# Queries of eight attention units loaded in 128-byte runs and turned by VectorE in SBUF instead of by TensorE

## The chip, the cores and the metric

The kernel runs on one core of a Trainium2 chip. The metric is device time in microseconds (us) of one execution. All engines of the core take part: TensorE (matmuls and, by a matmul with the identity, transposes), VectorE and ScalarE (elementwise work and the way out of PSUM), GpSimd and SyncE (which issue transfers to the 16 DMA engines).

## What is computed

Three stages follow one another: packed attention, a gated mixer, and a channel mixer. Cut to what matters:

```python
# attention, for each of 8 batches and 8 heads: q, k, v are [576, 64], p is [32, 64]
p_packed = sm_attn(p, k, v)                 # 32 packed rows look at all keys
out = sm_attn(q, p_packed, p_packed)        # every query looks at the 32 packed rows
# sm_attn(q, k, v): softmax(q k^T / sqrt(64)) v

# mixer on x = [8, 576, 512], x_prev = x moved down by one row
xk = mu_k * x + (1 - mu_k) * x_prev
xr = mu_r * x + (1 - mu_r) * x_prev
k = relu(xk @ w_k); v = (k * k) @ w_v; r = sigmoid(xr @ w_r); x = r * v

# channel mixer
u = x + (x^T @ U @ V)^T
out = u + relu(u @ w_ch1) @ w_ch2
```

## The kernel before

The kernel is written as a list of operations that a planner (`Plan`) puts in order. Each operation names its engine or engines, what it reads and writes, and a class. `emit` then runs through the list with a cost for each operation and hands every engine, whenever it is free, the ready operation of the lowest class; TensorE and SyncE take the oldest of a class, the others the one that was ready first. `copy` may go to ScalarE or to VectorE, whichever comes free for it first. The order that results is fixed in the program, and each engine runs its own list strictly in order. So a change of one step moves others around it. SyncE's list holds nearly all transfers; a transfer that waits for its data holds those behind it.

The attention is cut into 16 units. Unit u takes two heads (j = u % 4) of two batches (pair bp = u // 4). Units 0 to 7 (`NPLAIN = 8`, called plain) run at the start of the program, on four sets of buffers. Units 8 to 15 run on one set, one after another, beside the chunks of the mixer: the loop over chunks (n = 2 to 11; 384 columns each, three for each pair of batches) puts the units of pair 2 ahead of chunk 2 and those of pair 3 ahead of chunk 5. The pair's mixer chunks come only later, so the units are side work; the chunks' matmuls (`psr`, `psk`, `psv` for the products with w_r, w_k and w_v, `psu` for U) fill TensorE between their steps. Weights of the last stage are also loaded and prepared in the background there (`st`, `w_d`, class 3). From about 703 us on the last stage runs (`psc`, `psh`, `pst`).

A unit (`attention_steps`, L648) goes through these steps:

- k is turned by TensorE (`kin` to `kh`), scores of the packed rows are made (`sps`), and VectorE takes their maxima into `st` with two reductions; ScalarE takes exponentials into `a1`.
- q is turned. `load_q` (L621) brings q of both batches into `qin`, 128 partitions of 1152 values: partition 2p + b2 holds nine rows of both heads of batch b2. Two transfers of 288 KB do that, in runs of one row of a head, 64 values or 256 bytes. Then in three steps three blocks of 128x128 each are turned by TensorE into PSUM (bank `psat`), and a copy on ScalarE or VectorE brings each bank into `qt`, where a partition is a value of a head and the columns are the queries.
- the packed values (`pp`, `ppt`) are made from `a1` and v; `ppt` is multiplied with `qt`.
- units 8 to 15 (not plain) make this product with `ppt` as the stationary operand, so that the scores of 32 packed rows lie on partitions, and VectorE turns them with `turn` (L214, a stream transpose in blocks of 32x32) into `a2`; softmax over 32 follows, `turn` again into `qt`, and from there `th`, the product with `pp`, `xo`, and a store to `x_d`.

All big buffers of the set (`kin`, `qin`, `vin`, `kh`, `qt`, `at`, `th`, `xo`) come from one pool of eight in rotation, so each tile of a unit takes the place of the same tile, or another one, of the unit before. `load_k`, `load_q` and `load_v` of the next unit stand in the list right behind the steps that free their places.

Of the kernel before, what the change touches and what calls it, by code (L numbers as in the profile page):

```python
# [9 lines left out]
F32 = mybir.dt.float32  # L10
# [467 lines left out]
def packed_attention_moe_mixer_kernel(  # L478
# [18 lines left out]
    B, H, S, D = q.shape  # L497
    NP = p.shape[2]
    P = 128
# [3 lines left out]
    NI = S // 64  # L503
# [11 lines left out]
    NPLAIN = 8  # L515
# [4 lines left out]
    plan = Plan(nc)  # L520
# [37 lines left out]
    def ps_att():  # L558
        return plan.bank(att_banks[0], "psat", att_banks[0] is ps_a)
# [17 lines left out]
    class Bufs:  # L577
# [22 lines left out]
            return self.kept[1:]  # L600

        def tile_in(self, tag):
            return plan.tile(self.big_p, [P, 1152], F32, "big", parts=(0, 1, 2, 3), name=tag)

        def load_k(self, u, after=()):
            bp, j = divmod(u, NJ)
# [14 lines left out]
        def load_q(self, u, after=()):  # L621
            bp, j = divmod(u, NJ)
            if u not in self.qin:
                self.qin[u] = self.tile_in("qin")
            t = self.qin[u]
            for b2 in range(2):
                plan.dma(
                    t.at(b2)[b2:P:2, :].rearrange("p (i h d) -> p i h d", i=NI, h=2),
                    q[2 * bp + b2, 2 * j:2 * j + 2].rearrange("h (p i) d -> p i h d", i=NI), after=after)
# [18 lines left out]
    def attention_steps(A, u, u_next):  # L648
        bp, j = divmod(u, NJ)
        kin, qin, vin = A.kin.pop(u), A.qin.pop(u), A.vin.pop(u)  # L650
# [3 lines left out]
        plain = u < NPLAIN  # L654
        kh = A.big(F32, "kh")
        qt, at = A.big(F32, "qt"), A.big(F32, "at", (0, 1))
# [54 lines left out]
        for b2 in range(2):  # L711
            r = slice(b2 * 64, (b2 + 1) * 64)
# [2 lines left out]
        plan.reduce(s0[:, 8:9], s1[:, 4:8], add)  # L715
        plan.recip(s0[:, 9:10], s0[:, 8:9])

        for c in range(3):
            yield
            ps = ps_att()  # L720
            for t in range(3):
                i = 3 * c + t
                plan.transpose(ps[:, t * P:(t + 1) * P], qin[:, i * P:(i + 1) * P], ident)
            n = 3 if c < 2 or not plain else 2
            w = 8 if plain else NI
            plan.copy(
                qt[:, 0:w * P].rearrange("p (b i c) -> p i b c", b=2, i=w)[:, 3 * c:3 * c + n],
                ps[:, 0:n * P].rearrange("p (i c b) -> p i b c", i=n, b=2))
            if c == 2 and plain:
                plan.copy(qt[:, 1024:1152].rearrange("p (b c) -> p b c", b=2),  # L730
                          ps[:, 2 * P:3 * P].rearrange("p (c b) -> p b c", b=2))
        if early:
            A.load_q(u_next, A.after)

# [22 lines left out]
        if not plain:  # L757
            for b2 in range(2):
                r = slice(b2 * 64, (b2 + 1) * 64)
# [19 lines left out]
        if plain:  # L779
# [32 lines left out]
            for b2 in range(2):  # L812
                r = slice(b2 * 64, (b2 + 1) * 64)
                plan.copy(th[r, 512:576], ps[r, r])
        else:
            n = S // NP
# [24 lines left out]
        for c0, c1 in halves:  # L841
            w = c1 - c0
            if plain:
                yield
                pss = [ps_att() for _ in range(2)]
                for b2 in range(2):
                    r = slice(b2 * 64, (b2 + 1) * 64)
# [13 lines left out]
    def attention(A, u, u_next):  # L861
        for _ in attention_steps(A, u, u_next):
            pass
# [88 lines left out]
    for what in FIRST.split():  # L952
        u = int(what[1])
# [14 lines left out]
    plan.cls = 0  # L968
    A0.after = go
    steps = [attention_steps(lane[u], u, nxt[u]) for u in range(NLEAD)]  # L970
    prev = {w: u for u, w in nxt.items()}
    step = 0
# [47 lines left out]
    for b2 in range(2):  # L1020
        r = slice(b2 * 64, (b2 + 1) * 64)
# [7 lines left out]
    for i0, i1 in ((0, NI),):  # L1029
        src = uv[:, i0 * NP:i1 * NP]  # L1030
# [149 lines left out]
    def tmp_tile():  # L1180
        i = count["tmp"] % 6
        count["tmp"] += 1
        if i < 3:
            return plan.tile(m_p, [P, CW], F32, "m", name="tmp")[:, 0:256]
        return plan.tile(tr_p, [P, 256], F32, "tmp")
# [133 lines left out]
    def product(q, f, i, name, fresh):  # L1319

        if fresh:
            bank_abc[name] = plan.bank(ps_c1, "psc1")
        ps = bank_abc[name][:, 0:256]
        w, x = load_ws(f, i), ops[q][i]
        n = 0
        for k in range(2):
            for wi, a in PASS:
                plan.mm(ps, half(w, wi)[:, k * P:(k + 1) * P],
                        half(x, a).rearrange("p (a k c) -> p k a c", a=4, k=2)[:, k],
                        start=(fresh and n == 0), stop=(n == 5), skip_group_check=True)  # L1330
                n += 1
        return ps
# [78 lines left out]
    for n in range(2, len(chunks)):  # L1411
        b, c = chunks[n]
# [31 lines left out]
        if n >= CAST0:  # L1444
            plan.cls = 3
            for _ in range(len(casts) if n == NCAST else NPER):
                if casts:
                    rows, src, size, put = casts.pop(0)
# [27 lines left out]
    for q in range(NQ):  # L1476
# [11 lines left out]
        for f in range(NF):  # L1488
# [7 lines left out]
            b = product(q, f, 1, "b", True)  # L1496
            s = tmp_tile()
            plan.tt(s, p1, b, add)
            c = product(q, f, 2, "c", True)
# [67 lines left out]
```

## Time and profile before

| | us |
|---|---|
| median of 3 timed runs | 1484.77 |
| lowest and highest | 1484.17, 1485.76 |
| profiled execution, its own time | 1491.34 |
| span of its trace | 1489.6 |

Busy time in that span: TensorE 1461.4 us (matmuls) and 1277.7 us (weight loads), VectorE 980.2, ScalarE 728.3, GpSimd 270.3. Every count and duration from the trace belongs to this one execution; it took 6.6 us longer than the median of the timed runs.

Matmuls are pipelined: the duration of one in the trace is longer than the time by which it holds up the next, and the busy time of TensorE counts a stretch in which any of them runs. In the chain of waits, by contrast, pieces follow one another without overlap.

### The profile page before, as it was taken

Reading aid. Unit: us, or ns where it says so; the run is one execution under the profiler, and the core shown is the slowest. Engines: PE = TensorE matmul, PEld = TensorE weight load, DVE = VectorE, ACT = ScalarE, POOL = GpSimd, SP = SyncE. Lnnn points to the kernel's source line nnn. Section 1 sums busy time; section 2 is a strip of 40 time slices with the busy share of each in tenths; the row PEclk is TensorE's granted clock in tenths of the full one; section 3 lists DMA queues with packets and bytes.
Section 4 is the critical chain, followed back from the end, with each engine's and each line's share of the span. In section 5 each row is a group of like instructions: output and inputs, shape, how many; then the busy total and the mean of one; then the engine's idle time right before and its main releaser. Section 6 shows DMA issues by size and latency. Waiting matters only on the chain.

```text
span 1489.6 us, 25587 instructions
## 1 busy us (share of the span) xinstructions
PE 1461.4 (98%) x9208; PEld 1277.7 (86%) x9208; DVE 980.2 (66%) x2143; ACT 728.3 (49%) x1534; POOL 270.3 (18%) x522
## 2 busy tenths in 40 slices
PE   6999999999999999999999999999999999999998
PEld 5667888888888888889899999899999999999997
DVE  6677877788888888786855464545555555554533
ACT  5567656666666666676533233323333332333332
POOL 0000000000000000001333333333333333333331
PEclk9689999999999999999999999999999999999999
DMA  8863335654655446666988888888888878878763
GB/s 233 234 175 121 114 101 137 205 182 136 186 179 156 141 141 218 207 226 191 314 228 237 211 208 245 198 244 229 231 212 229 213 201 239 213 216 222 206 176 99
DMA packets 213708, 292.42 MB, mean 196 GB/s; under 512 B 70224, under 2 KB 105360, under 8 KB 213584
## 3 DMA queue, kind: packets, MB, share of 16 engines
q1 hardware_dynamic: 141008, 158.65, 34.7%
q0 software_dynamic: 72576, 132.15, 34.0%
q8 instruction: 74, 1.21, 0.3%
q14 instruction: 50, 0.41, 0.1%
HBM read 229.84 MB, written 60.89 MB: 195 GB/s over the span
## 4 chain that ended last, share of the span: by engine, by line
PE 92%; DMA 3%; DVE 2%; SPq 1%; ACT 1%; issue 1%; DVEq 0%
PE psc L197 50%; PE psk L197 13%; PE psv L197 12%; PE psr L197 7%; PE psat L197 5%; PE psat L209 3%; SPq L319 1%; PE psh L197 1%; PE psu L197 1%; DMA kin<-in_k_dram 1%; DMA s<-w_d 1%; DMA qin<-in_q_dram 0%; DMA x_d<-xo 0%; DMA prs<-x_d 0%; DVE ob L254 0%
## 5 line engine op out<-in xcount | busy, mean ns | idle before, releaser
L197 PE MATMUL psc<-w,hid 128*128 128x512 f32 x1728 | 420.7, 391 | 0.2 <-ACT xu L288 0.2
L197 PEld LDWEIGHTS psc<-ob,wb 128*128 128x128 f32 x3024 | 386.4, 191 | 15.1 <-ACT tmp L288 0.8
L197 PE MATMUL psc<-ob,wb 128*128 128x256 f32 x3024 | 391.1, 282 | 0.4 <-ACT tmp L288 0.4
L319 POOL DMA_DIRECT2D wb<-ws_d x504 | 267.3, 530 | 565.5 <-PE psc L197 436.9
L197 PEld LDWEIGHTS psc<-w,hid 128*128 128x128 f32 x1728 | 314.9, 188 | 60.7 <-DVE hid L273 0.7
L233 ACT ACTIVATE hid<-tmp 128x256 fp32r<-128x256 f32 x216 | 131.6, 676 | 229.8 <-DVE tmp L254 229.8
L197 PE MATMUL psk<-xk,wk 128*128 128x384 f32 x1056 | 208.4, 340 | 1.3 <-ACT sq L233 0.8
L197 PE MATMUL psv<-wv,kk 128*128 128x512 f32 x783 | 202.0, 395 | 0.0
L197 PEld LDWEIGHTS psk<-xk,wk 128*128 128x128 f32 x1056 | 184.6, 188 | 10.6 <-issue 1.5
L197 PEld LDWEIGHTS psv<-wv,kk 128*128 128x128 f32 x783 | 144.2, 188 | 28.3 <-issue 0.8
L273 DVE SCALAR_TENSOR_TENSOR hid<-tmp,hid 128x256 fp32r<-128x256 f32 x216 | 126.5, 631 | 49.8 <-ACT hid L233 48.3
L254 DVE TENSOR_TENSOR tmp<-tmp,psc 128x256 f32<-128x256 f32 x288 | 113.1, 410 | 64.4 <-PE psc L197 64.1
L273 DVE SCALAR_TENSOR_TENSOR hid<-psc,hid 128x256 fp32r<-128x256 f32 x72 | 45.3, 629 | 166.5 <-ACT hid L233 166.5
L233 ACT ACTIVATE hid<-psc 128x256 fp32r<-128x256 f32 x72 | 45.9, 637 | 147.9 <-PE psc L197 147.5
L197 PE MATMUL psr<-wr,xr 128*128 128x512 f32 x414 | 112.3, 404 | 0.1
L311 POOL MEMSET x<- 128x8 f32 x4 | 0.5, 113 | 538.4 <-DVE m L270 538.1
L197 PEld LDWEIGHTS psr<-wr,xr 128*128 128x128 f32 x414 | 75.8, 190 | 18.4 <-issue 3.2
L288 ACT ACTIVATE tmp<-psc 128x256 f32<-128x256 f32 x144 | 56.5, 392 | 54.1 <-PE psc L197 53.5
L233 ACT ACTIVATE sq<-psk 128x384 f32<-128x384 f32 x96 | 46.5, 490 | 66.0 <-PE psk L197 63.6
L254 DVE TENSOR_TENSOR kk<-sq,kk 128x384 fp32r<-128x384 f32 x87 | 47.8, 552 | 32.0 <-ACT kk L288 31.8
L270 DVE SCALAR_TENSOR_TENSOR m<-x,mu_t,m 128x384 f32<-128x384 f32 x88 | 51.6, 610 | 0.9 <-ACT m L233 0.9
L233 ACT ACTIVATE m<-x,om_t 128x384 f32<-128x384 f32 x88 | 50.8, 607 | 2.5 <-DVE xr L254 1.8
(176 smaller groups left out, 1645.9 us busy)
## 6 DMA issues: line engine op xcount, KB each, us to landing
wb<-ws_d POOLq DMA_DIRECT2D x504, 256.0 KB, 3.7
st<-in_moe_w_ch_dram SPq DMA_DIRECT2D x32, 512.0 KB, 5.3
ws_d<-wb SPq DMA_DIRECT2D x56, 256.0 KB, 3.0
qin<-in_q_dram SPq DMA_DIRECT2D x32, 288.0 KB, 5.7
x_d<-xo SPq DMA_DIRECT2D x16, 576.0 KB, 3.4
x_d<-x SPq DMA_DIRECT2D x36, 256.0 KB, 2.2
u<-x_d SPq DMA_DIRECT2D x36, 256.0 KB, 5.2
out_dram<-u SPq DMA_DIRECT2D x36, 256.0 KB, 3.2
```

The source lines that it names most:

```text
L197: self.nc.tensor.matmul(o, l, r, start=start, stop=stop, **k)
L209: self.nc.tensor.transpose(out.get(), in_.get(), ident.get())
L233: self.nc.scalar.activation(o, in_.get(), func, **k)
L254: return self.elem(engs, lambda e, o, x, y: e.tensor_tensor(out=o, in0=x, in1=y, op=op), out, [a, b], self.TT, cls)
L270: ("dve",), lambda e, o, x, y, z: e.scalar_tensor_tensor(out=o, in0=x, scalar=z, in1=y, op0=op0, op1=op1), out, [a, b, s], {"dve": (1.042, ...
L273: ("dve",), lambda e, o, x, y: e.scalar_tensor_tensor(out=o, in0=x, scalar=s, in1=y, op0=op0, op1=op1), out, [a, b], self.TT, cls)
L288: self.nc.scalar.activation(o, i, AF.Copy)
L311: (self.nc.gpsimd if eng == "pool" else self.nc.vector).memset(o, 0.0)
L319: (self.nc.sync if eng == "sp" else self.nc.gpsimd).dma_start(out=o, in_=i)
```

## The change

`load_q` fills `qin` otherwise for units 8 to 15. Four blocks of 32 partitions stand for head h and half e of its 64 values; partition r of a block holds, for each of 18 rows t, 32 values of row 18 r + t. Batch b2 takes 576 columns. Each of the eight combinations of b2, h and e is a transfer of its own (72 KB, 32 partitions of 18 runs of 32 values, 128 bytes). The three steps with TensorE's transposes and copies remain for plain units alone. For the others two `turn` operations of 128x576 on VectorE, one for each batch, turn every block of 32x32 from `qin` into `qt`; they write every second element, so that the queries come in the same order as before.

```diff
         def tile_in(self, tag):
-            return plan.tile(self.big_p, [P, 1152], F32, "big", parts=(0, 1, 2, 3), name=tag)
+            return plan.tile(self.big_p, [P, 1152], F32, "big", parts=tuple(range(8)), name=tag)
...
             t = self.qin[u]
+            if u >= NPLAIN:
+                for b2 in range(2):
+                    for h in range(2):
+                        src = q[2 * bp + b2, 2 * j + h].rearrange("(r t) (e s) -> e r t s", t=2 * NI, e=2)
+                        for e in range(2):
+                            g = 2 * h + e
+                            plan.dma(t.at(2 * g + b2)[g * 32:(g + 1) * 32, b2 * S:(b2 + 1) * S]
+                                     .rearrange("p (t s) -> p t s", s=32), src[e], after=after)
+                return
...
-        for c in range(3):
+        for c in range(3 if plain else 0):
             yield
             ps = ps_att()
             for t in range(3):
                 i = 3 * c + t
                 plan.transpose(ps[:, t * P:(t + 1) * P], qin[:, i * P:(i + 1) * P], ident)
-            n = 3 if c < 2 or not plain else 2
-            w = 8 if plain else NI
+            n = 3 if c < 2 else 2
             plan.copy(
-                qt[:, 0:w * P].rearrange("p (b i c) -> p i b c", b=2, i=w)[:, 3 * c:3 * c + n],
+                qt[:, 0:8 * P].rearrange("p (b i c) -> p i b c", b=2, i=8)[:, 3 * c:3 * c + n],
                 ps[:, 0:n * P].rearrange("p (i c b) -> p i b c", i=n, b=2))
-            if c == 2 and plain:
+            if c == 2:
...
+        if not plain:
+            yield
+            for b2 in range(2):
+                r = slice(b2 * S, (b2 + 1) * S)
+                plan.turn(qt[:, r].rearrange("p (i r e) -> p e i r", i=NI, e=2), qin[:, r])
```

The planner's list changes on all engines. Three places matter for what follows. The first is TensorE's list where unit 9 turns its q, a piece of the difference (`psat<-ident,qin` are the turns of q, `psk` and `psv` are matmuls of the chunk):

```order
 L197 MATMUL psk<-xk,wk_0_204 128x384 x3
-L197 MATMUL psk<-xk,wk_0_205 128x384 x2
-L209 MATMUL psat<-ident,qin 128x128 x3
-L197 MATMUL psk<-xk,wk_0_205 128x384
-L197 MATMUL psk<-xk,wk_0_206 128x384 x3
-L197 MATMUL psk<-xk,wk_0_207 128x384 x3
-L209 MATMUL psat<-ident,qin 128x128 x3
-L197 MATMUL psv<-wv_1872,kk 128x512 x2
-L209 MATMUL psat<-ident,qin 128x128 x3
+L197 MATMUL psk<-xk,wk_0_205 128x384 x3
+L197 MATMUL psk<-xk,wk_0_206 128x384 x3
+L197 MATMUL psk<-xk,wk_0_207 128x384 x3
```

The nine turns are gone, and the matmuls of the chunk stand next to each other. All 72 turns of units 8 to 15 are gone from the list; the 72 of units 0 to 7 stay.

The second is VectorE's list at the maxima of unit 8's scores (`st_152<-psat`), the list before:

```order
L277 TENSOR_REDUCE st_152<-psat_2762 128x1
L254 TENSOR_TENSOR xs_2761<-x2_2556,xs_2761 128x512
L277 TENSOR_REDUCE st_152<-psat_2763 128x1
L254 TENSOR_TENSOR kk_2699<-sq_2641,kk_2699 128x384
L261 TENSOR_SCALAR st_152<-st_152 128x1
```

and now:

```order
L277 TENSOR_REDUCE st_152<-psat_2774 128x1
L254 TENSOR_TENSOR xs_2773<-x2_2556,xs_2773 128x512
L215 STREAM_TRANSPOSE qt_2709<-qin_2675 128x2x288
L277 TENSOR_REDUCE st_152<-psat_2775 128x1
L254 TENSOR_TENSOR kk_2705<-sq_2641,kk_2705 128x384
L215 STREAM_TRANSPOSE qt_2709<-qin_2675 128x2x288
L261 TENSOR_SCALAR st_152<-st_152 128x1
```

Unit 8's two turns of q stand between its two maxima and behind the second. The third place is SyncE's list where the loads of unit 10 stand (`x` is the next chunk's input, `st` and `w1_d`, `w2_d` are weights of the last stage), the list before:

```order
L319 DMA x_d2_67<-xo_2912 128x1152
L319 DMA x_3151<-x_d1_66 128x4x512
L319 DMA kin_3168<-in_k_dram 128x2x256 x2
L319 DMA kin_3168<-in_k_dram 64x2x64 x2
L319 DMA w1_d0_78<-m_2776 128x512
L319 DMA st_3054<-in_moe2_w_ch2_dram 128x1024
L319 DMA st_3196<-in_moe2_w_ch1_dram 128x4x256
L319 DMA w2_d0_102<-m_2925 128x512
L319 DMA qin_3323<-in_q_dram 64x18x64 x2
```

and now:

```order
L319 DMA x_d2_67<-xo_2917 128x1152
L319 DMA kin_3159<-in_k_dram 128x2x256 x2
L319 DMA kin_3159<-in_k_dram 64x2x64 x2
L319 DMA qin_3160<-in_q_dram 32x18x32 x8
L319 DMA x_3179<-x_d1_66 128x4x512
L319 DMA w1_d0_78<-m_2788 128x512
L319 DMA st_3022<-in_moe2_w_ch2_dram 128x1024
```

q of unit 10 moved up from behind the weights to right behind k, and the chunk's input and the weights stand behind its eight transfers.

## Rows read from the trace of the kernel before

**Rows 1.** The page's head: busy time by engine, granted clock of TensorE in tenths by slice
```profile
PE 1461.4 (98%) x9208; PEld 1277.7 (86%) x9208; DVE 980.2 (66%) x2143; ACT 728.3 (49%) x1534; POOL 270.3 (18%) x522
...
PEclk9689999999999999999999999999999999999999
```

**Rows 2.** Busy time (and instructions) by stretch, then clock, DMA share, GB/s
```profile
239.00:493.00 254.00, 252.12 (x1735) 212.75 (x1734) 213.25 (x472) 172.18 (x378) 0.11 (x1) 1.00 0.53 163
690.00:730.00 40.00, 39.43 (x220) 34.28 (x219) 28.68 (x55) 24.02 (x48) 7.99 (x16) 1.00 0.75 233
```

**Rows 3.** The chain of waits from 239 to 493 us, shares by line
```profile
by line: PE psv L197 31.4%; PE psk L197 28.1%; PE psr L197 15.7%; PE psat L197 11.3%; PE psat L209 8.2%; PE psu L197 2.5%; ACT L233 1.0%; ACT r L233 0.7%; DVE xs L254 0.3%; issue 0.3%; ACT a L233 0.3%; ACT r L288 0.2%; ACT sq L233 0.2%; DVE
```

**Rows 4.** TensorE's waits from 200 to 520 us: total, times, longest
```profile
PE psu L197 <- DVE xs L291: 1.0, 2, 0.5
PE psu L197 <- DVE xs L254: 0.4, 1, 0.4
PE psk L197 <- ACT sq L233: 0.4, 1, 0.4
```

**Rows 5.** Groups of instructions from 239 to 493 us on TensorE: busy us, mean ns
```profile
L209 PE MATMUL psat<-ident,qin 128*128 128x128 f32 x72 | 11.6, 272 | 0.0
```

**Rows 6.** The chain from 236 to 250 us: start us, us, what
```profile
238.14 1.61 PE psv L197 x7
239.76 0.33 PE psat L209 x3
240.08 0.47 PE psv L197 x2
...
240.91 0.66 PE psat L209 x6
241.56 0.70 PE psk L197 x4
```

**Rows 7.** Tile qt from 200 to 560 us: duration ns min/median/max, first and last start
```profile
L288 ACT ACTIVATE qt<-psat x15: 486/491/496, 241.3 to 492.9; 128x384 f32<-128x384 f32 x15
L291 DVE COPY qt<-psat x9: 539/558/560, 240.1 to 459.2; 128x384 f32<-128x384 f32 x9
L215 DVE STREAM_TRANSPOSE qt<-a x8: 770/772/773, 257.6 to 509.0; 128x576 f32<-128x576 f32 x8
```

**Rows 8.** Line 215, all stream transposes, the group of the last stage
```profile
L215 DVE STREAM_TRANSPOSE ux<-u x32: 677/690/712, 725.9 to 1366.7; 128x512 f32<-128x512 f32 x32
```

**Rows 9.** Tile qin from 200 to 520 us: its issues on SyncE, their landing
```profile
L319 SPq DMA_DIRECT2D qin<-in_q_dram x16: 607/682/2368, 221.9 to 459.2; - x16
...
DMA to landing us min/median/max: 3.9/6.1/9.2
```

**Rows 10.** SyncE in order of time from 218 us: start us, us, what
```profile
221.95 1.40 SPq L319 DMA_DIRECT2D qin<-in_q_dram  x2
227.02 0.35 SPq L319 DMA_DIRECT2D x_d<-x  x1
...
232.32 2.27 SPq L319 DMA_DIRECT2D qin<-in_q_dram  x2
234.70 1.90 SPq L319 DMA_DIRECT2D x_d<-x  x1
```

**Rows 11.** DMA from 315 to 318 us, 40 slices in tenths; packets
```profile
DMA  6699999999999999999999999999999998988988
...
DMA packets 2294, 0.75 MB, mean 251 GB/s; under 512 B 2066, under 2 KB 2294, under 8 KB 2294
```

**Rows 12.** VectorE in order of time from 233.3 us, the maxima of unit 8
```profile
233.39 0.49 DVE L277 TENSOR_REDUCE st<-psat 128x1 f32<-128x320 f32 x1
...
234.40 0.42 DVE L277 TENSOR_REDUCE st<-psat 128x1 f32<-128x256 f32 x1
```

**Rows 13.** The chain from 660 to 735 us, at the handover
```profile
701.55 0.45 PE pst L209 x4
...
716.44 8.21 DMA s<-w_d
```

## Prediction

> **What bounds the kernel now.** I read the page's head first, then the stretch in which the changed units run, then the chain of waits there, and last the queues that the change touches. The head [rows 1] shows TensorE busy over 98% of the span, at a granted clock of nine tenths or more, the 2.4 GHz level, from the fourth slice on. A busy share of matmuls says little by itself, because matmuls overlap, so the next view is the stretch from the first to the last turn of q of the changed units, 239 to 493 us [rows 2]: TensorE leaves 254 - 252.1 = 1.9 us unused, VectorE is busy 213 us (84%), ScalarE 172 us (68%), the DMA engines 53%, and the clock is 1.00. The chain by line [rows 3] says the same in another way: TensorE's lines make up more than 95% of that stretch. TensorE's own waits between 200 and 520 us come to 1.8 us [rows 4]. So in this stretch, TensorE's stream of instructions is what ends last, and an instruction taken out of it comes out of the time as long as nothing else moves up.
>
> How long is one of these instructions on that path? The group of the 72 turned blocks gives a mean of 272 ns [rows 5], but that is the time from issue to end of one pipelined instruction. The chain [rows 6] shows what each holds up: three take 0.33 us and six take 0.66 us, so 0.11 us each, while the matmuls around them keep their pace (psv 1.61 / 7 = 0.23 us before and 0.47 / 2 = 0.235 us after; psk 0.18 us). I take 0.11 us.
>
> **The change, part by part.**
>
> TensorE: 8 units (8 to 15) lose 9 turns each, 72 x 0.11 = **7.9 us off the path**. The weights of each turn go with it and lie inside the 0.11 us. The 72 turns of units 0 to 7 stay.
>
> Copies out of PSUM: 24 go, 15 on ScalarE at 491 ns (7.4 us) and 9 on VectorE at 558 ns (5.0 us) [rows 7]. They lie beside TensorE's work, so they are worth nothing on the path, and 24 fewer requests for the two banks that attention shares give at most a little of the 1.8 us that TensorE waits.
>
> VectorE: 16 turns of 128x576 come in. The trace has the same shape from SBUF to SBUF, 772 ns [rows 7], writing in order; the new ones write every second element. A turn that writes so is there too, 128x512 at 690 ns [rows 8]: 1.35 ns an element against 1.34, so the stride costs nothing and I take 772 ns, 12.4 us in all. VectorE's net load is 12.4 - 5.0 = +7.4 us, if nothing else moves: 220.6 of 246 us, 90% in place of 84%. The order shows that the planner moves some casts to ScalarE besides. Cover: TensorE's stream. Its price is bounded below by 0 and above by 7.4 us (every added microsecond is waited for); VectorE ends 1.4 of TensorE's 1.8 us of waits [rows 4], so I take +0.4 us.
>
> SyncE's queue: 16 loads become 64, 48 more issues. One holds the queue 0.68 us in the median [rows 9]; the new ones have half the partitions and a run more per row, so I keep that: 33 us over the stretch, 4 us a unit. What stands behind them there are v of the unit, the cast loads, the next x and the stores. Bounds: 0 (the queue has idle time, such as 223.4 to 227.0 us, where it waits for a store's data [rows 10]) and 33 us. The nearest place is that one: six more issues of unit 8 (4.1 us) fill the 3.6 us of idling, and what follows shifts by about half a microsecond there and some 3 us after unit 9. I take 0 on the path.
>
> DMA engines: bytes stay, packets of q double, from 2,304 to 4,608 a unit, 18,432 more. In three microseconds in which q's runs make up most of the traffic and the engines don't rest, 2,294 packets pass, 2,066 of them under 512 bytes [rows 11]: 1.31 ns of all 16 engines for each. Were the price per packet, 18,432 more cost 24 us; were it per byte, 0. I take the packets' price for the share, which then rises from 53% to (0.53 x 254 + 24) / 246 = 64%; a load that is asked for a unit ahead doesn't notice that, so 0 on the path.
>
> The Trainium skill (DMA: Bandwidth & Descriptors, "Specifications") says that a transfer needs runs of 512 bytes for the full rate and that below it the engine reads, changes and writes back. That speaks against runs of 128 bytes; both the old 256 and the new 128 lie below its limit, so by it the per-packet end (24 us of engine time) is the right one and the sum does not change. No row here shows 128-byte runs.
>
> The one new wait at the head of a queue: VectorE's turn of unit 8 stands between the two maxima of its scores (the order above shows it), which run at 233.4 and 234.4 us [rows 12]. Its q is issued from 221.95 us [rows 10]; eight issues of 0.68 us end at 227.4 us, and a landing takes 3.9 to 9.2 us, 6.1 in the median [rows 9], so 231.3 to 236.6, 233.5 us in the median, against a turn at about 234.4. If late, VectorE stands up to 2.2 us; queued behind it are the second maximum and the unit's bias, a kk remainder and a cast of psu's operand. Between 0 and 2.2 us, once; I take +0.3. From unit 10 on q is asked for right behind k, a unit ahead, and no turn can be late by it.
>
> Sum: -7.9 + 0.4 + 0 + 0 + 0.3 = **-7.2 us**. What comes behind shifts as a whole. Where the chunks hand over to the last stage, between 690 and 730 us, TensorE is busy 39.4 of 40 us [rows 2]; the chain leaves it at 702 us for VectorE's operands and a load of 8.2 us, but that leg starts from turns of TensorE's own (pst) and so comes earlier with them [rows 13]. No fixed time stands there that could take the gain back. Against the profiled execution that is 1491.34 - 7.2 = 1484.1 us; the median of the timed runs lies 6.6 us lower, and the same difference from it gives 1484.77 - 7.2 = **1477.6 us**.
>
> **The rivals.**
>
> 1. VectorE becomes the engine that ends last. It gains 7.4 us where TensorE loses 7.9, so the time would stay: 1484.8 - 7.9 + 7.4 = 1484.3 us. For it: 84% busy and strictly in order, in a stretch with short bursts of full load. Against it: it ends 1.4 us of TensorE's waits in 320 us, and part of its load is casts of weights that nobody awaits soon. It decides once more than about 5 of the 7.4 us are waited for. A half effect, 3.7 us, gives 1480.6.
>
> 2. The turns on TensorE were not on the bound at all, because weight loads are busy only 213 of 254 us [rows 2] and 16% of the stretch is free: time unchanged, 1484.8 us. Against it stands the chain [rows 6], in which the next matmul starts 0.33 us later for three turns; a 512-column matmul streams for 0.23 us, during which a load has time to wait. The Trainium skill (Perfetto Trace Analysis, "Identifying the Most-Contended Engine") wants TensorE judged by the busy share of weight loads and not by that of matmuls. By that rule alone, 84% would leave room; the chain does not agree that it is room for these turns.
>
> 3. Slower: SyncE's queue. Its 33 us more of issue time stand ahead of the cast loads, of the x of the next chunk (behind q of unit 10 in the new order) and of v. ScalarE and VectorE take each cast in order, so a cast load that lands late holds the copies that free TensorE's banks. The gain is gone when a quarter (7.9 of 33 us) reaches TensorE; with half, 16.4 us, the time is 1484.8 - 7.9 + 16.4 = 1493.3 us. For it: eight loads per unit in one burst, and 4 us a unit. Against it: the queue waits for data in long spells, and before the change none of TensorE's waits goes back to a DMA [rows 4].
>
> That the change doesn't do what it says is ruled out by the order: the 72 turns are gone from TensorE's list.
>
> **How the numbers follow.** Forecast (gain of 5 to 10 us, 1474.8 to 1479.8): 0.68. Half of rival 1 (gain of 3 to 5 us, 1479.8 to 1481.8): 0.10. Rivals 1 in full and 2 (within 3 us either way): 0.14. Rival 3: 0.08. Timed runs here spread by 0.1%, and 0.2%, 3 us, is about what a measurement of this kernel can tell from no change. So faster 0.78, same 0.14, slower 0.08. The forecast's ends are all 72 turns with a little of TensorE's own waits on top (-10 us) and rival 1 at half (1480.6); with the part of rivals 1 and 2 next to it, the range that leaves out 2 in 10 is 1474.5 to 1483 us.
>
> **What would show it.** In the changed profile: no turn of qin on TensorE after 200 us, 16 turns qt from qin on VectorE near 772 ns, TensorE idle still about 2 us between 239 and 486 us, and the last turns of u before the last stage (pst, 701.55 us now [rows 13]) some 7 us earlier. VectorE at about 90% there with TensorE idle by more than 5 us would be rival 1; ScalarE or VectorE waiting for st or x loads by more than 5 us in sum, rival 3. A first turn of unit 8 that waits for qin beyond 235 us would show the head-of-queue wait. I am wrong if TensorE's idle time in the stretch grows by more than 3 us.

## The result and the profile after

| | before | after |
|---|---|---|
| median of the timed runs, us | 1487.01 (6 runs: 1484.17 to 1492.78) | 1502.12 (6 runs: 1499.05 to 1504.66) |
| profiled execution / span, us | 1491.34 / 1489.6 | 1504.66 / 1502.9 |

The changed kernel is slower: ratio 1.0102, 95% interval 1.0082 to 1.0122, some 15 us where 7 fewer were forecast. The page's head, which answers to [rows 1], shows TensorE busy for 6.7 us less than before, as the missing turns would have it, and yet a dip at the handover that was not there, in the twentieth of the 40 slices (714 to 751 us), in its busy time and in its granted clock:

```profile
PE 1454.7 (97%) x9136; PEld 1270.0 (85%) x9136; DVE 982.9 (65%) x2133; ACT 725.6 (48%) x1534; POOL 269.5 (18%) x522
...
PE   6799999999999999999699999999999999999998
...
PEclk8889999999999999999799999999999999999999
```

The two stretches of [rows 2], and then the handover in slices of 10 us (columns: TensorE busy and instructions, weight loads, VectorE, ScalarE, GpSimd, granted clock, DMA share, GB/s):

```profile
239.00:493.00 254.00, 250.40 (x1727) 209.15 (x1726) 216.12 (x469) 174.25 (x379) 0.11 (x1) 1.00 0.55 161
690.00:730.00 40.00, 30.70 (x153) 25.15 (x152) 29.90 (x59) 15.93 (x32) 9.81 (x19) 0.87 1.05 328
...
710.00:720.00 10.00, 5.01 (x22) 3.15 (x21) 7.30 (x14) 2.26 (x4) 1.06 (x2) 0.86 1.15 370
720.00:730.00 10.00, 6.27 (x20) 4.49 (x20) 5.32 (x8) 3.15 (x5) 0.83 (x2) 0.62 1.12 359
730.00:740.00 10.00, 5.10 (x32) 4.63 (x31) 5.62 (x9) 4.58 (x8) 1.80 (x4) 0.89 1.21 308
740.00:750.00 10.00, 10.00 (x51) 8.90 (x51) 7.72 (x16) 6.31 (x12) 2.64 (x5) 0.77 1.02 298
```

Where the units run, TensorE is nearly as full as before: 3.6 of 254 us unused, against 1.9. At the handover it leaves 9.3 of 40 us unused, against 0.6, and after the first gap its granted clock falls (a mean of 0.62 in 720 to 730 us, so part of it at 1.2 GHz) and is at 0.77 even in 740 to 750, where TensorE is busy without a break.

Three places on SyncE part the program into stages, and this table carries most of what follows: the first store of a mixer result to `x_d` (start of the chunks), the first such store of the last chunk, and the first store of the output.

| us | start of the chunks | chunks | handover | last stage |
|---|---|---|---|---|
| before | 215.2 | 497.2 | 87.6 | 689.6 |
| after | 213.0 | 491.5 (-5.8) | 108.1 (+20.5) | 690.3 |

The chunks took 5.8 us less; the handover took 20.5 us more. The start lies anywhere from 206 to 218 us in the profiled executions of this study, for kernels whose work ahead of it is the same, so I compare the lengths of stages and not the ends. Each length comes from one execution: e2 below, whose time is that of before, repeats them within 0.2 us for the chunks and the handover, but the two differences together part from the timed one by some 4 us in several runs and by 7 us in e8.

What TensorE waited for from 600 to 800 us in the changed kernel (total, times, longest); before, two waits of 0.4 and 0.2 us stood there:

```profile
PE psh L197 <- DVE u L254: 5.0, 3, 2.7
PE psc L197 <- ACT tmp L288: 4.9, 1, 4.9
PE psc L197 <- ACT w L288: 3.7, 1, 3.7
PE psc L197 <- DMA wb<-ws_d: 0.6, 1, 0.6
```

VectorE and ScalarE are mostly messengers. The chain of waits, which answers to [rows 13], shows what stands behind them, transfers one after the other:

```profile
706.86 8.69 DMA x_d<-x
...
717.60 6.95 DMA s<-w_d
...
724.57 5.65 DMA ut<-uq_d
...
730.28 7.46 DMA s<-w_d
...
738.73 26.29 PE psc L197 x146
```

The first is the store of the last chunk's own result. Two of the other three are `s<-w_d`, weights of the last stage (`load_w2`). The views leave numbers out, so `w_d` stands for both of its matrices, `w1_d` and `w2_d`. They are made ready in three steps: casts in the background, class 3, store both to `w_d`; `make_ws`, class 3 too, loads the first again (`raw`), combines its blocks and stores them to `ws_d`; `load_w2`, class 1, loads the second (`s`) through the same five buffers as `raw`, behind it. These buffers open only when the last cast and the last attention unit are done. SyncE's instructions on `w_d` (duration ns min/median/max, first and last start), and how long ScalarE, which makes `w` from `s`, waited for such a load (us, times), before:

```profile
L319 SPq DMA_DIRECT2D w_d<-m x32: 319/333/546, 271.1 to 570.9; - x32
L319 SPq DMA_DIRECT2D raw<-w_d x16: 327/430/1092, 573.2 to 674.4; - x16
L319 SPq DMA_DIRECT2D s<-w_d x16: 319/352/481, 683.4 to 728.8; - x16
...
  ACT w L288: 1.8, 5
```

and after:

```profile
L319 SPq DMA_DIRECT2D w_d<-m x32: 319/341/975, 273.8 to 587.4; - x32
L319 SPq DMA_DIRECT2D raw<-w_d x16: 319/424/1136, 589.6 to 687.4; - x16
L319 SPq DMA_DIRECT2D s<-w_d x16: 319/338/577, 717.1 to 744.9; - x16
...
  ACT w L288: 13.8, 8
```

The chunks came 8 us sooner at their end, and the last cast 16.5 us later, the first `raw` 16.4 us later, the first `s` 33.7 us later. TensorE's first product with `w` starts at 724.6 us, against 714.4 us before. Not all of its waits are for weights: the 5.0 us for `u` are waits between blocks of the next group (`psh`), which it ran at 712 to 721 us while no `w` was there. In SyncE's list the delay is seen without any clock: ahead of the store of chunk 8's result, 32 of 32 casts were stored and 3 `raw` loads issued before, and 30 and none after; ahead of the last chunk's first store, 8 `s` loads were issued before, and none after.

### The profile page after: what moved, and what is told of

Read it like the earlier page. It is cut to its first block, busy times and chain, and to the rows that moved or that the text cites. A ratio compares the mean times of both kernels' runs of the same rounds, so it can differ in the third digit from the quotient of the medians.

```text
span 1502.9 us, 25510 instructions
## 1 busy us (share of the span) xinstructions
PE 1454.7 (97%) x9136; PEld 1270.0 (85%) x9136; DVE 982.9 (65%) x2133; ACT 725.6 (48%) x1534; POOL 269.5 (18%) x522
## 3 DMA queue, kind: packets, MB, share of 16 engines
q1 hardware_dynamic: 160208, 158.65, 34.9%
## 4 chain that ended last, share of the span: by engine, by line
PE 89%; DMA 5%; DVE 2%; ACT 2%; SPq 1%; issue 1%; DVEq 0%; ACTq 0%
PE psc L197 49%; PE psv L197 13%; PE psk L197 13%; PE psr L197 7%; PE psat L197 4%; PE psat L209 2%; SPq L319 1%; DMA kin<-in_k_dram 1%; DMA s<-w_d 1%; PE psu L197 1%; PE psh L197 1%; DMA ut<-uq_d 1%; DMA qin<-in_q_dram 1%; DMA x_d<-x 1%; DMA st<-in_moe_w_v_dram 0%
## 5 line engine op out<-in xcount | busy, mean ns | idle before, releaser
L233 ACT ACTIVATE hid<-psc 128x256 fp32r<-128x256 f32 x72 | 45.8, 636 | 153.1 <-PE psc L197 153.0
```

What stands on the lines that cost most here:

```text
L233: self.nc.scalar.activation(o, in_.get(), func, **k)
```

## The experiments

The theories. **L**: the planner made its list anew, gave the turns on VectorE the places in which background casts had run, and the last stage's weights were late. **S**: the 48 more loads on SyncE hold the queue (the prediction's third rival). **C**: chunks that end sooner leave the background less time, whatever the planner does. **T**: the turns cost VectorE more than they free on TensorE (the first rival). The first three runs take the change apart, the next five move the background or the planner, the last keeps the planner out of it. Their stages, in us, with the difference from before, and how far ahead of the last chunk's first store the first `s` load is issued (before 29.0 us ahead; in the changed kernel 12.6 us behind):

| run | chunks | handover | first `s` | timed ratio, 95% |
|---|---|---|---|---|
| e1: turns on VectorE, old loads | 489.9 (-7.3) | 108.4 (+20.7) | 11.2 behind | 1.0107, 1.0082 to 1.0132 |
| e2: new loads, turns on TensorE | 497.0 (-0.2) | 87.7 (+0.1) | 29.0 ahead | 1.0006, 0.9991 to 1.0021 |
| e3: no turns of q | 487.9 (-9.3) | 90.1 (+2.5) | 16.5 ahead | 0.9983, 0.9967 to 0.9998 |
| e4: casts in class 1 | 505.7 (+8.5) | 89.3 (+1.7) | 27.1 ahead | 1.0090, 1.0068 to 1.0112 |
| e5: before, casts spread later | 496.5 (-0.7) | 126.8 (+39.2) | 33.9 behind | 1.0264, 1.0245 to 1.0284 |
| e6: preparation from chunk 7 in class 1 | 495.9 (-1.3) | 90.4 (+2.8) | 48.7 ahead | 0.9987, 0.9974 to 1.0001 |
| e7: casts from chunk 5 in class 1 | 502.1 (+4.9) | 90.1 (+2.5) | 27.1 ahead | 1.0068, 1.0049 to 1.0086 |
| e8: the planner's price of one kind of operation | 499.6 (+2.4) | 91.2 (+3.6) | 18.5 ahead | 1.0089, 1.0072 to 1.0106 |
| e9: the change in the list of before | 490.5 (-6.7) | 88.8 (+1.2) | 29.0 ahead | 0.9966, 0.9952 to 0.9980 |

The handover and the first `s` go together: where it comes 16 us ahead or more, the handover takes at most 3.6 us more than before; where it comes 11 to 13 us behind, in e1 and the changed kernel, some 20 us more, and at 34 us behind, in e5, 39 us.

**e1, the turns without the loads.** The kernel before with two turns of 128x576 on VectorE in place of nine on TensorE and three copies; q is loaded as before.

```diff
-        for c in range(3):
+        for c in range(3 if plain else 0):
...
+        if not plain:
+            yield
+            for b2 in range(2):
+                r = slice(b2 * S, (b2 + 1) * S)
+                plan.turn(qt[:, r].rearrange("p (i r e) -> p e i r", i=NI, e=2), qin[:, r])
```

> The kernel before with one half of the change: the two loads of 288 KB in 256-byte runs stay, but VectorE turns q (16 turns of 128x576) and TensorE's 72 turns are gone. The columns of q then come out of the turns in a wrong order, so the scores of the queries are not the reference's; every instruction of the changed kernel but the 64 loads is there. Theory L (the preparation of the last stage's weights, which the planner gives the lowest class, is pushed back against the chunks by VectorE's turns, and TensorE waits for it at the handover): ratio to before 1.007 to 1.013, first load of raw about 590 us, TensorE idle 10 to 17 us between 700 and 750 us. Rival S (the 64 loads on SyncE's queue hold up the loads of the weights): ratio 0.993 to 0.997, first raw load about 565 to 573 us, no idle at the handover.

Measured 1500.05 us, ratio 1.0107. The whole loss is there with the old two loads of 256-byte runs. S falls; L and C stand.

**e2, the loads without the turns.** `load_q` and `tile_in` as in the change, and nothing else.

```diff
+            if u >= NPLAIN:
+                for b2 in range(2):
+                    for h in range(2):
...
+                            plan.dma(t.at(2 * g + b2)[g * 32:(g + 1) * 32, b2 * S:(b2 + 1) * S]
```

> The kernel before with the other half of the change: q of units 8 to 15 comes in eight loads of 128-byte runs, and TensorE turns it as before (the layout does not fit, so the queries' scores are not the reference's). Theory L: ratio 0.998 to 1.002, first load of raw at about 573 us, TensorE idle under 2 us between 690 and 740 us. Rival S: ratio 1.005 to 1.015, raw at 585 us or later, TensorE idle over 8 us at the handover.

Measured 1486.1 us, ratio 1.0006. Eight loads in place of two cost nothing that can be measured. SyncE's issues of `qin` and their landing, from 200 to 520 us, to be read against [rows 9]:

```profile
L319 SPq DMA_DIRECT2D qin<-in_q_dram x64: 566/630/2311, 216.3 to 458.9; - x64
...
DMA to landing us min/median/max: 2.5/3.2/6.5
```

An issue takes 0.63 us instead of 0.68, and a load lands in 3.2 us instead of 6.1.

**e3, no turns of q at all.** The 72 turns and 24 copies are left out, and GpSimd fills `qt` with zeros.

```diff
-        for c in range(3):
+        for c in range(3 if plain else 0):
...
+        if not plain:
+            yield
+            plan.zero(qt[:, 0:1152])
```

> The kernel before without any turn of q in units 8 to 15: TensorE's 72 turns and the 24 copies are left out, GpSimd fills qt with zeros instead, the loads of q stay as before. So q does not enter the result of these units. It shows what the missing TensorE work gives alone. Theory L in its strict form (VectorE's added work is the cause): VectorE has 5 us less to do, the weights come in time, ratio 0.993 to 0.996. Rival C (the chunks end sooner, so the background work has less time, whoever turns q): the weights come late all the same, ratio 1.000 to 1.010, TensorE idle over 5 us at the handover. Rival S: 0.993 to 0.996.

The chunks end sooner than in the changed kernel, by 9.3 us against before, and the handover is 2.5 us longer, not 20.5. So C, that chunks which run faster starve the background, explains little of the loss. It does explain a part of the delay: ahead of chunk 8's store 31 casts are stored and no `raw` is issued, and 12 of the 29 us of the first `s` load's lead are gone. What takes the rest of the lead in e1 comes with the 16 operations on VectorE and the list made for them. The ratio lies between the ranges expected of L and of C. The timed gain of 2.5 us is less than that of the two stages together (6.8 us); the profiled execution was the fastest of ten (1477.58 us, the median 1483.67), and why is open.

**e4, casts in class 1.** The changed kernel, in which the casts are no longer background.

```diff
         if n >= CAST0:
-            plan.cls = 3
+            plan.cls = 1
```

> The changed kernel with one number changed: the casts of the last stage's weights beside the chunks get class 1 of the planner instead of class 3, the same as the chunks' work, so they keep their place among it. Theory L: the first load of raw comes at about 565 us, the handover has under 2 us of idle TensorE, and the 72 turns' gain shows: ratio 0.992 to 0.997. Rival S (loads late): the loads stay late, ratio 1.005 or more. Rival C: less time for the background is made good by its better class, so the same as L; C and L part in the run without turns.

The handover is whole again, and the time is not: 1498.04 us, not the gain expected of L. The stretch from 210 to 540 us, in the columns of [rows 2]:

```profile
210.00:540.00 330.00, 319.78 (x2070) 266.13 (x2069) 267.47 (x572) 218.62 (x475) 0.11 (x1) 0.99 0.54 162
```

The first of TensorE's waits from 200 to 540 us:

```profile
PE psat L197 <- ACT ppt L288: 2.7, 1, 2.7
PE psat L209 <- DVE pp L270: 1.6, 3, 0.6
PE psr L197 <- ACT r L288: 1.2, 2, 1.0
```

TensorE now leaves 10 us unused among the chunks (3.6 in the changed kernel), waiting for many small steps of ScalarE and VectorE. That casts, now of the same class, stand ahead of these steps is my reading of it. The loss has only moved.

**e5, late background alone.** The kernel before, with four casts asked for at a chunk instead of five, so that more of them come last.

```diff
-    CAST0, NPER = 2, 5
+    CAST0, NPER = 2, 4
```

> The kernel before, with TensorE's turns and the old loads, and one number changed: four casts of weights per chunk instead of five (NPER), so that the background work falls behind the chunks without anything of the change. In its list, 37 of the 56 prepared pieces (ws_d) are stored ahead of the last chunk's result, and no load of w2, where the kernel before has 56 and 8 and the changed kernel 54 and 0. Theory L (the loss is the late preparation, however it came to be late): slower, ratio 1.012 to 1.035, TensorE idle over 15 us between 690 and 760 us. Rival T (VectorE's turns themselves cost the time, in the stretch where they run): ratio 0.998 to 1.003.

Measured 1527.71 us, ratio 1.0264. Nothing of the change is in this kernel, and its chunks take no longer than before. Its first `raw` is issued at 633.4 us, and TensorE's waits from 600 to 850 us are:

```profile
PE psc L197 <- ACT w L288: 12.5, 1, 12.5
PE psc L197 <- DMA wb<-ws_d: 12.4, 2, 10.9
```

The stretch from 690 to 750 us there:

```profile
690.00:750.00 60.00, 33.17 (x145) 25.46 (x144) 44.97 (x102) 24.85 (x60) 7.02 (x13) 0.73 0.93 291
```

So a late background is enough to make such a loss. What TensorE waits for are weights of the last stage, as in the changed kernel: `w` in both, and here the `ws_d` loads as well, for which it waits only 0.6 us there. The clock falls too, to 0.73 in the mean of this stretch.

**e6 and e7, parts of the preparation in class 1.** In the changed kernel, e6 moves the casts from chunk 7 on and `make_ws` (the diff), e7 the casts from chunk 5 on alone (`n >= 5`, and `make_ws` stays in class 3).

```diff
         if n >= CAST0:
-            plan.cls = 3
+            plan.cls = 1 if n >= 7 else 3
...
         if n > NCAST:
-            plan.cls = 3
+            plan.cls = 1
```

> The changed kernel with the planner's class 1 instead of 3 for the preparation of the weights behind the last attention unit only: the casts of chunks 7 and later and the products of weights (make_ws) after them; the casts beside the attention keep class 3. In its list all 56 pieces and 8 loads of w2 stand ahead of the last chunk's result, as in the kernel before. Theory L: the handover has under 4 us of idle TensorE, and what the 72 turns give shows, ratio 0.993 to 0.998, 1477 to 1484 us. Rival T: 1.004 to 1.010. With the earlier run of class 1 for all casts in mind (1.009): if the class itself holds up the chunks, TensorE idles between 540 and 690 us instead.

> The changed kernel with class 1 for the casts from chunk 5 on and class 3 before and for the products of weights. Its list has the same background progress as the kernel before from chunk 7 on (28 and 32 casts, 56 pieces, 8 loads). Theory L: no idle TensorE at the handover, ratio 0.993 to 1.000; casts of class 1 beside units 12 to 15 may cost up to half of what the class cost for all chunks (10 us of idle TensorE between 210 and 540 us there). Rival T: 1.004 to 1.010.

Both repair the handover (+2.8 and +2.5 us). e7 shows that earlier casts alone do it, and pays among the chunks as e4 did (+4.9 us): its ratio, 1.0068, lies in the range named for T. e6 takes back the loss: 1484.36 us against 1502.12 in the changed kernel, a ratio to before of 0.9987 with an interval that holds 1. The chunks' gain is down to 1.3 us there, so e6 undoes the harm and does not bring the forecast.

**e8, the planner's price.** In the changed kernel the planner takes VectorE's operations on two operands, and its reductions, for 4 ns shorter each. The work is the same.

```diff
-    TT = {"dve": (1.042, 154.0), "pool": (2.084, 158.0)}
+    TT = {"dve": (1.042, 150.0), "pool": (2.084, 158.0)}
```

> The changed kernel with the planner's fixed cost of one VectorE operation 150 instead of 154 (a number of the planner alone, no instruction changes, the order does). In its list 56 pieces and 10 loads of w2 stand ahead of the last chunk's result, where the changed kernel has 54 and 0. Theory L: since the list decides, ratio 0.994 to 1.003. If the change is bad whatever the list (rival T): 1.007 to 1.013.

The handover is nearly repaired (+3.6 us), and the expectation of L is missed all the same: 1501.2 us, a ratio within the range named for T, with 2.4 us lost among the chunks. Its background is late too at first, with 30 casts and no `raw` load ahead of chunk 8's store, as in the changed kernel, but ten `s` loads stand ahead of the last chunk's. Of the 10.4 us between its span and that of before, a late start of the chunks (217.8 us) makes up 2.6 and the last stage 1.8. Of the timed loss, some 13 us by the ratio, these two stages hold 6 us; where the rest lies I did not settle. What it does show is that a list made anew moves the stages by several us with no change in the work.

**e9, the change without a new list.** The planner's decisions for the kernel before (order on each engine, choice of engine, choice of bank) are written down and followed. Two turns of a unit stand on VectorE where the first and fourth turn stood on TensorE, and eight loads where two stood.

```diff
-        while True:
-            best = None
...
+        for op, e in line:
+            held.append((op, e))
...
+TURN_AT = (1, 6)
```

> The changed kernel, with nothing planned anew: the planner is replaced by the list that it made for the kernel before (which instruction comes next on each engine, which engine takes it, which bank). Every instruction that both kernels have stands where it stood before, the stores and loads of the last stage's weights included; the eight loads of a unit stand where its two stood, the 72 turns of TensorE and the 24 copies are gone, and the two turns of a unit stand on VectorE where the first and the fourth turn of the unit stood on TensorE. Theory L (the loss comes from the order that the planner made anew, with the background work of the last stage later against the chunks): the handover stays as in the kernel before (some 88 us from the first store of the last chunk's x to the first output, 108 in the changed kernel), and the stretch of the chunks keeps the gain that the prediction worked out, 5 to 8 us; the ratio comes out at 0.994 to 0.997, 1477 to 1482 us. Its rival, that the turns cost VectorE more than they free on TensorE whatever the order (VectorE over 90% busy in 240 to 490 us, with TensorE waiting for it): the chunks' stretch is no shorter than before, the ratio is 0.999 or more.

Measured 1482.35 us (12 runs, 1478.72 to 1484.13) against 1487.87, ratio 0.9966, interval 0.9952 to 0.9980: faster than both kernels. The two stretches of [rows 2]:

```profile
239.00:493.00 254.00, 251.75 (x1700) 210.99 (x1699) 225.13 (x495) 172.83 (x369) 0.11 (x1) 1.00 0.58 170
690.00:730.00 40.00, 38.62 (x231) 33.81 (x231) 33.16 (x64) 23.08 (x44) 11.13 (x21) 1.00 0.97 288
```

TensorE's waits from 200 to 540 us, which answer to [rows 4]:

```profile
PE psu L220 <- DVE xs L314: 1.0, 2, 0.5
PE psu L220 <- DVE xs L277: 0.4, 1, 0.4
PE psk L220 <- ACT sq L256: 0.4, 1, 0.4
PE psv L220 <- DVE kk L277: 0.3, 1, 0.3
```

SyncE's instructions on `w_d`:

```profile
L342 SPq DMA_DIRECT2D w_d<-m x32: 319/333/1160, 263.7 to 557.8; - x32
L342 SPq DMA_DIRECT2D raw<-w_d x16: 326/432/2355, 560.1 to 661.4; - x16
L342 SPq DMA_DIRECT2D s<-w_d x16: 319/320/544, 670.4 to 716.6; - x16
```

VectorE is busy 225 of 254 us, 89%, and TensorE waits 0.3 us more than before in that stretch, not several, and the chunks take 6.7 us less: T falls, for which the ratios of e7 and e8 had spoken. The background moves forward with the chunks (last cast 13.1 us sooner than before, of which 6.3 us is the earlier start), and the handover takes 1.2 us more, not 20.5. The same work in the two lists differs by 20 us. With e5, e6 and e7, which only ask for the background at another place or in another class, L is confirmed in its main part: the new list, and in it the late weights. How the planner came to push them back is less sure. In the stretch up to the store of chunk 6's result it stores 19 casts where the list of before stores 21, as if the turns had taken their places; but e3, with no turns on VectorE, stores 20 there.

## Why the prediction was wrong

The step that failed is the last one of the sum: "What comes behind shifts as a whole" and "No fixed time stands there that could take the gain back". It took the last leg of the chain at the handover [rows 13] as tied to TensorE's own turns. The load of 8.2 us in that leg, `s<-w_d`, is tied to something else, a preparation that has a pace of its own. The last turns of `u` ahead of that leg did come 7.3 us earlier, as foretold (694.25 against 701.55 us), and the load did not come with them. In the kernel before, the first `s` load stands 29 us ahead of the last chunk's first store (683.4 against 712.4 us); after, it stands 12.6 us behind it (717.1 against 704.5). What the prediction held against its first rival, that part of VectorE's load is "casts of weights that nobody awaits soon", overlooked that deadline. The sum priced the turns by their waits at TensorE and left out what their time on VectorE was taken from. The order shown ahead of the prediction had a sign of it: the cast loads stand further back in SyncE's list at unit 10. I read that for the time of the issues and did not follow the weights to those who need them.

The terms one by one:

- TensorE, -7.9 us: held. With +0.4 and +0.3 the sum was -7.2; the chunks took 5.8 us less in the changed kernel, 7.3 in e1 and 6.7 in e9. e3, with nothing on VectorE in return, gives 9.3. The Trainium skill (Perfetto Trace Analysis, "Identifying the Most-Contended Engine") judges TensorE's headroom by MFU, which no view here shows, and by the busy share of weight loads; by that share the stretch had room and the turns would have been free. e9 does not agree: weight loads are busy 211 of 254 us there, and the chunks still took 6.7 us less.
- Copies out of PSUM, 0: they go in e1, e3 and e9 together with the turns, and no run parts them.
- VectorE's turns: 772 ns forecast, 772 measured (rows below). TensorE's waits from 200 to 540 us rose from 1.8 to 3.6 us in the changed kernel, and to 2.1 in e9, for +0.4 forecast. VectorE was to be at about 90%; it was at 85% in the changed kernel and 89% in e9. That shortfall goes with the casts that were put off. In 254 us counted from 23.8 us behind the start of the chunks, VectorE was given 7.4 us more work and its busy time rose by 2.5 us, from 213.3 to 215.7; 19 casts are stored there where 21 were, and a cast takes some 2.9 us of VectorE. In e9, with 21 casts, its busy time rises to 222.9.
- SyncE, 0 out of 33 us: held, e2. An issue takes 0.63 us, so 30 us came, and none of it was awaited.
- DMA engines, 0 on the path: held, e2. Of the 24 us of engine time, taken from the price per packet, about 10 came, as an estimate: by the pages' rows on the queues, the packets of SyncE's queue took 35.5% of 1485.2 us in e2, 527.2 us, against 34.7% of 1489.6 us, 516.9 us, with the same bytes and 19,200 packets more (141,008 before, 160,208 in e2), 0.54 ns each. The Trainium skill (DMA: Bandwidth & Descriptors, "Specifications") lets every run below 512 bytes pay for reading, changing and writing back; whatever these runs paid, it did not reach the time.
- Unit 8's turn at the head of VectorE's queue, +0.3: nothing came of it. The first turn starts at 232.2 us, ahead of the 235 us that would have shown it late, and no idle time stands ahead of any of the 16.

The tile `qin` of the changed kernel from 200 to 520 us, its loads and its turns; a row under the last line would name what VectorE had waited for, and there is none:

```profile
L319 SPq DMA_DIRECT2D qin<-in_q_dram x64: 565/630/1509, 219.9 to 447.2; - x64
L215 DVE STREAM_TRANSPOSE qt<-qin x16: 767/772/781, 232.2 to 468.2; 128x576 f32<-128x576 f32 x16
its engine sat idle before it (us, times) until:
```

The rivals: none of the three happened. The one with slower at its end named the casts, but with the wrong cause, the issue time of SyncE, which e2 shows to be worth nothing, and the wrong effect, copies that free TensorE's banks too late instead of weights that the last stage lacks. That the time came out on its side is luck.

What the handover lost adds up from rows: TensorE is idle for 14.2 of 60 us from 690 to 750 us, against 0.6 before, which is 13.6 us; and 45.8 us of work at a mean granted clock of 0.86 is 6.4 us less than at full clock, as an estimate. That is 20.0 of 20.5 us.

## What to carry to other kernels

Where a planner orders the program, an edit is two edits, the work and a new list, and the second can cost more than the first gives: here -6.7 us and +20 us. Before a gain is counted, follow each background chain to its deadline and read how far ahead of it it runs, in the list made anew too. A count of background steps at a fixed place of the main work shows it without a clock, if it is taken at the end of the chain: ahead of the last chunk's store no `s` load is issued in the three kernels with the loss at the handover, and eight or more in all others. The count at chunk 8 misleads, as e8 shows. To learn what the work alone is worth, run it in the old list.

## What the runs showed of the hardware

A turn of 128x576 that writes every second element takes the same 772 ns as one that writes in order [rows 7]. Loads of 72 KB in runs of 128 bytes landed in 3.2 us in the median (e2), where the 288 KB in runs of 256 bytes took 6.1 [rows 9], and an issue of a quarter of the bytes took 0.63 us against 0.68. The granted clock fell in the gaps of the handover and came back late: 0.62 in 720 to 730 us, where TensorE was busy 6.3 of 10 us, and still 0.77 in 740 to 750 us, in which it never rested.
